# Sums of weight blocks kept in half tiles: four writes a pair instead of eight, and a new order for the whole program

## The chip, the core and the metric

The kernel runs on one core of a Trainium2 chip. The metric is the device time of one execution in microseconds (us). A NeuronCore has five engines, each with its own queue of instructions that it works through in order: TensorE (PE, matmuls), VectorE (DVE), ScalarE (ACT), GpSimd (POOL) and SyncE (SP, which here only issues DMA transfers). Engines wait for one another through semaphores. An instruction that waits holds up everything behind it on its queue.

## The reference, cut to what matters

```python
# q, k, v: (8, 8, 576, 64); w_in: (512, 2048); w_out: (2048, 512)
q_s = exp(q - max(q, -1)); q_s /= sum(q_s, -1) + 1e-9        # softmax over the head's width
k_s = exp(k - max(k, 2));  k_s /= sum(k_s, 2) + 1e-9         # softmax over the sequence
x   = q_s @ (k_s^T @ v)                                      # linear attention, per head
h   = x.reshape(4608, 512) @ w_in
g   = h * tanh(softplus(h))                                  # Mish
out = g @ w_out
```

All of it is in 32-bit floats. The kernel multiplies in a reduced matmul format (fp32r): every operand is split into a high part and a low part, and a product is three matmuls (high x high, high x low, low x high).

## The kernel before, in words

**Stages.** The 4608 rows of x are cut into nine blocks of 512. The first three blocks are multiplied plainly: for each of 16 slices f of the hidden width, `HM` (twelve matmuls of 512 columns, tile `ph`) makes h, `Y` applies Mish, `GA` and `GL` split it into `gh` and `gl`, and `OP` (four parts of three matmuls, tiles `po`) adds to the output. Step number n = 16 x block + f, so `HM16` begins the second block. The last six blocks are done in three rounds (k = 0, 1, 2) of two, by a scheme that makes a 2 x 2 block product with seven block multiplications instead of eight. `Ak.n.p` is one first product (six matmuls) and `BBk.f.p` one second product (six matmuls); `C`, `J`, `N` take results out of PSUM into tiles `g`; `GX` forms differences of such tiles, `GH` and `GK` split them for the second product. `XA`, `XH`, `XL` do the same to x.

**The weights' sums.** The scheme needs, beside the weight blocks themselves, sums and differences of them (products p = 5, 6, 7 and 3). All blocks are written once, in the order in which they will be used, to a scratch tensor `ws` in HBM, and fetched from there in each round by `F` (512 KB each, issued by POOL into a ring of six tiles; two products use up one tile). From the second plain block to the first part of round 0 the kernel fills `ws`:

- `WKj` (16 of them) writes three blocks as they are: three writes of 256 KB on SP, from tiles `wi` or `wo`.
- `WWj` (POOL, two additions) makes the whole values of the pair j of weight tiles, in a tile `w_in` or `w_out` of which there is one buffer only (tag `raw`).
- `WMj` (POOL, four additions of 256 columns) makes the four sums in a tile `m_in` or `m_out` (tag `st`, two buffers).
- `WHj` (ACT) rounds the four sums to their high part and puts it where the whole values stood; `WLj` (DVE) leaves the low part in `m`.
- `WPj` writes them: for each of the four sums its high part and its low part apart, eight writes of 128 KB on SP.

Pairs 0 to 7 are of w_in, 8 to 15 of w_out (`w_out5` is pair 13).

**Attention beside it.** Heads come in pairs. For a pair of tiles, SP loads k (`LK`, tile `kt_two`), v (`V`) and q (`LQ`, one buffer, so a load waits until `EQ` has read the one before). DVE takes the maximum of k (`MK`, tile `km`) and of q (`MQ`, tile `qm`); POOL subtracts (`SQ`) and normalizes (`QM`, tile `qe`); DVE joins sums (`QV`) and transposes q (`T`, tile `qT`); PE multiplies q with the pair's k^T v (`PX`) and makes the next pair's k^T v (`PK`). `ES` and `ST` write finished outputs and leftovers of x.

**What sets the order.** Every engine's order is the order of tokens in two long strings, `FIRST` and `LATER`, which a planner wrote; nothing is reordered afterwards. The tiles `g` of the rounds lie in the memory of the tiles `wo`, so `C0.2.3`, which writes the memory of `wo7`, has to wait for `WW15`, which reads `wo7`.

Of the kernel before, what the change touches and what calls it, by code (L numbers as in the profile page):

```python
# [46 lines left out]
UE8.1 GL16 OP14.0 U8.1 OP14.1 WK5 OP14.2 Y17 LK10 OP14.3 WK9 QW8 HM18g GA17 QV8 WK15 MS9 GL17 QM8 WH0 WK7 MT9 PK6ef T8
SQ9 Y18 WK10 OP15.0 GA18 WL0 OP15.1 V10 OP15.2 EV0.0v WP0 EQ9 OP15.3 GL18 EV0.1s HM19h Q9 EV0.2v QW9 LQ10 MK10 ES0.0
EV0.3s WK12 OP16.0 QV9 OP16.1 OP16.2 WK13 S8 QM9 Y19 OP16.3 KB10 MQ10 ES0.1 WW1 HM20g GA19 T9 MS10 GL19 KM10 OP17.0
WK14 WM1 OP17.1 ES0.2 OP17.2 UE10.0 OP17.3 UE10.1 HM21h MT10 U10.0 SQ10 U10.1 Y20 ES0.3 WH1 LK12 OP18.0 OP18.1 GA20  # L50
WL1 Y21 OP18.2 OP18.3 GL20 WP1 PX8ef EQ10 HM22g GA21 Q10 Z8 LQ11 GL21 Z9 ZL8 QW10 ZL9 QV10 PK8ef WW2 MK12 Y22 OP19.0
V12 ZT8 GA22 ST8 OP19.1 MQ11 ZT9 OP19.2 KB12 ST9 GL22 QM10 OP19.3 MS11 S10 HM23h WM2 OP20.0 Y23 OP20.1 MT11 T10 SQ11
WH2 OP20.2 OP20.3 GA23 KM12 WL2 HM24g GL23 WP2 EQ11 UE12.0 Q11 OP21.0 QW11 U12.0 OP21.1 LQ12 QV11 OP21.2 QM11 OP21.3
Y24 HM25h T11 WW3 UE12.1 MQ12 GA24 U12.1 OP22.0 MS12 OP22.1 GL24 LK14 WM3 OP22.2 OP22.3 Y25 PX10ef GA25 HM26g MT12 WH3
GL25 SQ12 Z10 WL3 Z11 OP23.0 ZL10 WP3 OP23.1 ZL11 EQ12 OP23.2 MK14 OP23.3 HM27h LQ13 Q12 Y26 KB14 GA26 KM14 QW12 GL26
PK10ef WW4 Y27 OP24.0 V14 OP24.1 OP24.2 UE14.0 QV12 WM4 OP24.3 GA27 MQ13 HM28g ZT10 ZT11 ST10 GL27 MS13 ST11 S12
UE14.1 QM12 WH4 OP25.0 OP25.1 MT13 WL4 OP25.2 OP25.3 Y28 SQ13 T12 WP4 HM29h GA28 U14.0 GL28 EQ13 U14.1 OP26.0 LQ14 Q13
LK16 OP26.1 OP26.2 Y29 OP26.3 WW5 QW13 HM30g GA29 QV13 WM5 OP27.0 GL29 Y30 OP27.1 MQ14 GA30 OP27.2 GL30 MS14 OP27.3
MK16 QM13 HM31h WH5 WL5 KB16 T13 WP5 OP28.0 Y31 OP28.1 MT14 KM16 GA31 SQ14 OP28.2 GL31 OP28.3 PX12ef UE16.0 HM32g EQ14
XR12 LQ15 Q14 WW6 XR13 QW14 OP29.0 UE16.1 OP29.1 PK12ef F0 QV14 WM6 MQ15 Y32 OP29.2 V16 ZT12 S14 OP29.3 GA32 ST12  # L60
# [15 lines left out]
C0.0.0 XL0.4 OP47.0 OP47.1 SQ21 T20 A0.0.7 EV2.0v F6 J0.0.0 ES2.0 WW13 A0.0.6 EQ21 EV2.1s LQ22 OP47.2 C0.0.2 ES2.1
OP47.3 KM22 F7 A0.1.1 Q21 WM13 EV2.2v N0.0.0 A0.1.2 ES2.2 QW21 MQ22 C0.1.0 A0.0.5 EV2.3s F8 QV21 WH13 ES2.3 A0.1.7 F9
J0.1.0 QM21 C0.0.3 A0.1.6 MS22 F10 WL13 F11 T21 WP13 UE22.0 J0.0.3 PX20df C0.1.2 U22.0 A0.0.3 UE22.1 MT22 SQ22 XR20
U22.1 A0.0.4 XR21 LK24 EQ22 A0.2.1 F12 J0.0.2 LQ23 WW14 Q22 A0.2.2 N0.0.1 C0.2.0 A0.1.5 QW22 J0.2.0 F13 N0.1.0 QV22
A0.2.7 WM14 N0.2.0 MQ23 C0.1.3 MK24 A0.2.6 MS23 N0.0.2 A0.1.3 J0.1.3 KB24 F14 MT23 QM22 WH14 PK20df C0.2.2 KM24 F15  # L80
WL14 A0.1.4 N0.1.1 V24 ZT20 SQ23 T22 ZT21 WP14 A0.3.1 J0.1.2 UE24.0 A0.3.2 S22 F16 C0.3.0 ST20 U24.0 A0.2.5 EQ23 ST21
J0.3.0 UE24.1 LQ24 A0.3.7 Q23 F17 U24.1 WW15 A0.3.6 N0.3.0 LK26 QW23 MQ24 C0.3.2 N0.1.2 F18 QV23 WM15 C0.2.3 MS24
J0.2.3 A0.2.3 N0.0.3 A0.2.4 N0.1.3 N0.2.1 MT24 QM23 MK26 WH15 A0.4.1 F19 N0.2.3 J0.2.2 A0.4.2 SQ24 C0.4.0 T23 KB26
A0.3.5 F20 J0.4.0 WL15 A0.4.7 EQ24 KM26 WP15 C0.3.3 Q24 PX22df F21 UE26.0 J0.3.3 A0.4.6 QW24 XR22 QV24 A0.3.3 LQ25
XR23 QM24 C0.4.2 A0.3.4 F22 PS PK22df N0.3.1 J0.3.2 GH0.1.0 MQ25 A0.5.1 V26 T24 MS25 A0.5.2 ZT22 F23 MT25 C0.5.0 S24
ST22 SQ25 ZT23 A0.4.5 GH0.1.1 ST23 GK0.1.0 A0.5.7 F24 J0.5.0 GX0.0.0p EQ25 A0.5.6 U26.0 C0.4.3 LQ26 Q25 UE26.1 A0.4.3
J0.4.3 C0.5.2 F25 U26.1 QW25 A0.4.4 GK0.1.1 LK28 A0.6.1 F26 J0.4.2 N0.4.1 GX0.1.0p N0.4.0 A0.6.2 C0.6.0 N0.5.0 A0.5.5
N0.2.2 F27 QV25 GH0.1.2 A0.6.7 J0.6.0 QM25 C0.5.3 MQ26 A0.6.6 N0.6.0 J0.5.3 F28 MS26 T25 A0.5.3 N0.3.2 GK0.1.2 C0.6.2
A0.5.4 N0.4.2 F29 MT26 N0.5.1 GX0.0.1v N0.3.3 A0.7.1 N0.4.3 SQ26 J0.5.2 N0.5.3 A0.7.2 MK28 C0.7.0 F30 GX0.2.0p PX24df
A0.6.5 EQ26 XR24 LQ27 GX0.1.1v A0.7.7 XR25 F31 C0.6.3 J0.7.0 A0.7.6 J0.6.3 N0.5.2 A0.6.3 Q26 F32 C0.7.2 MQ27 N0.7.0  # L90
A0.6.4 GX0.2.1v N0.6.1 GH0.1.3 BB0.0.1 F33 J0.6.2 QW26 GK0.1.3 PK24df MS27 QV26 BB0.1.1 N0.6.2 V28 MT27 ZT24 QM26 S26
ZT25 ST24 KB28 A0.7.5 ST25 GH0.2.0 KM28 F34 T26 SQ27 BB0.2.1 C0.7.3 GK0.2.0 BB0.3.1 F35 UE28.0 J0.7.3 A0.7.3 GH0.2.1
U28.0 A0.7.4 EQ27 GK0.2.1 F36 LQ28 BB0.4.1 Q27 N0.7.1 J0.7.2 BB0.5.1 QW27 GX0.3.0p N0.7.2 BB0.6.1 N0.6.3 GH0.2.2 F37
QV27 BB0.7.1 F38 N0.7.3 GK0.2.2 BB0.0.2 QM27 UE28.1 BB0.1.2 F39 GX0.3.1v GH0.2.3 BB0.2.2 GH0.7.0 T27 BB0.3.2 GK0.2.3
DP0.0.0 F40 DP0.0.1 GK0.7.0 XH1.1 BB0.4.2 GH0.7.1 U28.1 BB0.5.2 F41 GX0.0.2v LK30 PX26df GH0.7.2 GK0.7.1 BB0.6.2 XR26
# [897 lines left out]
```

## Time and profile before

| | |
|---|---|
| median of three runs | 835.33 us (834.29 to 836.96) |
| the profiled execution | 835.84 us, of it 834.1 us span from first to last instruction |
| mean granted TensorE clock | 0.981 of full speed |
| busy: PE, DVE, ACT, POOL | 797.3, 518.5, 536.4, 338.1 us |
| HBM read and written | 138.19 and 39.85 MB |

Shares of the span are means over stages with different limits. The plain blocks end and the rounds begin at about 336 us; a PE that is "busy" has a matmul under way, so what matters for the end is each stretch in which PE stands still, and who ended it. In the views, a name such as `DVE gl L218` is an instruction by its engine, the tile that it writes and its line; L218 is a helper's line, shared by many. `SPq` is SP's queue; the time of an SP entry is the time it took to issue, not to land.

### The profile page before, as it was taken

To read this page: it belongs to the slowest core of one execution; us is meant where nothing else is said; L and a number is where in the kernel's file an instruction comes from. 1 tells how busy PE (TensorE), PEld (TensorE's weight loads), DVE (VectorE), ACT (ScalarE), POOL (GpSimd) and SP (SyncE) were. 2 spreads that over 40 slices of the span, in tenths; PEclk is the share of its full clock that TensorE was granted. 3 is DMA by queue.
4 is the path that set the end of the run, shared out by engine and by line. 5 is a ranking of instruction groups with operands and counts; after the bars stand their busy time and mean duration, and the time that the engine had idled before them with its cause. 6 is when DMAs were issued, how large, how long until landed. Compare 5 with 4: busy or idle time off the path is not lost.

```text
span 834.1 us, 12849 instructions
## 1 busy us (share of the span) xinstructions
PE 797.3 (96%) x4654; PEld 639.6 (77%) x4654; DVE 518.5 (62%) x804; ACT 536.4 (64%) x962; POOL 338.1 (41%) x391
## 2 busy tenths in 40 slices
PE   9899999399999999896999999999999999999998
...
PEclk9999999699999999988999999999999999999999
...
GB/s 343 392 325 146 56 129 332 341 206 144 132 223 138 134 152 100 274 264 250 262 217 223 261 189 254 251 195 195 205 201 210 217 232 205 195 201 183 221 198 180
DMA packets 85758, 178.87 MB, mean 214 GB/s; under 512 B 16576, under 2 KB 45248, under 8 KB 85696
## 3 DMA queue, kind: packets, MB, share of 16 engines
...
HBM read 138.19 MB, written 39.85 MB: 213 GB/s over the span
## 4 chain that ended last, share of the span: by engine, by line
PE 77%; DMA 7%; SPq 5%; ACT 4%; POOL 3%; DVE 2%; issue 2%; POOLq 0%; ACTq 0%; DVEq 0%
PE px L805 13%; PE ph L619 12%; PE qx L822 12%; PE po L657 11%; PE qz L822 8%; PE qy L822 8%; PE py L805 7%; SPq L693 4%; PE pz L805 3%; PE px L524 1%; DMA kt<-in_kt_dram 1%; POOL m_out L725 1%; DMA raw_x<-in_w_dram 1%; DMA ws<-w_out 1%; POOL w_out L715 1%
## 5 line engine op out<-in xcount | busy, mean ns | idle before, releaser
L788 POOL DMA_DIRECT2D ws<-ws x172 | 93.2, 542 | 299.1 <-PE qx L822 66.8
L855 ACT CAST gs<-g 128x1024 fp32r<-128x1024 f32 x84 | 88.3, 1052 | 85.4 <-PE qx L822 38.7
L805 PE MATMUL px<-xh,ws 128*128 128x512 f32 x384 | 134.0, 397 | 7.9 <-ACT g L833 7.9
L218 DVE TENSOR_TENSOR gs<-g,gs 128x1024 fp32r<-128x1024 f32 x84 | 105.1, 1251 | 45.3 <-ACT gs L855 44.9
L657 PE MATMUL po<-wo,gh 128*128 128x512 f32 x384 | 119.6, 393 | 0.0
L822 PE MATMUL qx<-gs,ws 128*128 128x512 f32 x432 | 100.7, 389 | 0.0
L619 PE MATMUL ph<-xs,wi 128*128 128x512 f32 x384 | 96.8, 399 | 1.3 <-ACT qT L516 1.2
L805 PEld LDWEIGHTS px<-xh,ws 128*128 128x128 f32 x384 | 73.3, 191 | 28.1 <-ACT g L833 8.7
L822 PEld LDWEIGHTS qx<-gs,ws 128*128 128x128 f32 x432 | 81.0, 188 | 16.9
L619 PEld LDWEIGHTS ph<-xs,wi 128*128 128x128 f32 x384 | 71.8, 191 | 19.6 <-issue 2.0
L657 PEld LDWEIGHTS po<-wo,gh 128*128 128x128 f32 x384 | 71.2, 188 | 18.1 <-issue 3.2
L805 PE MATMUL px<-xl,ws 128*128 128x512 f32 x192 | 75.7, 394 | 0.0
L657 PE MATMUL po<-wo,gl 128*128 128x512 f32 x192 | 74.7, 389 | 0.0
L841 ACT ACTIVATE g<-g 128x512 f32<-128x512 f32 x72 | 44.8, 631 | 44.8 <-DVE g L837 44.4
L837 DVE TENSOR_TENSOR g<-py,g 128x512 f32<-128x512 f32 x48 | 32.9, 684 | 63.7 <-PE py L805 48.7
L805 PE MATMUL py<-xh,ws 128*128 128x512 f32 x192 | 68.3, 397 | 0.0
L822 PE MATMUL qy<-gs,ws 128*128 128x512 f32 x288 | 67.2, 389 | 0.0
L822 PE MATMUL qz<-gs,ws 128*128 128x512 f32 x288 | 67.0, 389 | 0.0
L822 PEld LDWEIGHTS qz<-gs,ws 128*128 128x128 f32 x288 | 54.0, 188 | 12.0 <-issue 0.8
L619 PE MATMUL ph<-xs_odd,wi 128*128 128x512 f32 x192 | 48.8, 405 | 14.9 <-DVE gl L218 14.9
L833 ACT COPY g<-px 128x512 f32<-128x512 f32 x72 | 41.9, 582 | 32.9 <-PE px L805 28.6
L822 PEld LDWEIGHTS qy<-gs,ws 128*128 128x128 f32 x288 | 54.0, 188 | 11.2
...
## 6 DMA issues: line engine op xcount, KB each, us to landing
...
v<-in_v_dram SPq DMA_DIRECT2D x14, 594.0 KB, 4.6
...
kt_two<-in_kp_dram SPq DMA_DIRECT2D x12, 576.0 KB, 4.3
q<-in_qs_dram SPq DMA_DIRECT2D x24, 288.0 KB, 3.4
ws<-wi SPq DMA_DIRECT2D x24, 256.0 KB, 3.7
ws<-wo SPq DMA_DIRECT2D x24, 256.0 KB, 4.1
out_dram<-ob SPq DMA_DIRECT2D x24, 256.0 KB, 3.8
```

The source lines that it names most:

```text
L218: eng.tensor_tensor(out, a, b, ALU.subtract)
L524: nc.tensor.matmul((px, pt)[x][h][o], kvt[a, j], at[e + j]["qT"][x][a], start=True, stop=True)
L619: nc.tensor.matmul(gs[n], wi[f][:, a, t], x[:, z], start=t == 0 and i == 0, stop=t == HP - 1 and i == 2)
L657: nc.tensor.matmul(po[t], g[a][:, t * P:(t + 1) * P], wo[f][:, z], start=f == 0 and i == 0, stop=f == NF - 1 and i == 2)
L693: nc.sync.dma_start(dst if z is None else dst[:, z], src)
L788: nc.gpsimd.dma_start(t.rearrange("p s z j c -> p s (z j c)"), ws[e % (NW // 2)].bitcast(F32R))
L805: nc.tensor.matmul(dst, w[:, a, j], xc[k, p][z][:, j].rearrange("p b s -> p (b s)"), start=p in (1, 2, 7) and j == 0 and i == 0, stop=j == ...
L822: nc.tensor.matmul(psb[key, k][m], w[:, a, m], g[:, z, f % 2], start=first and i == 0, stop=f == NH - 1 and i == 2, skip_group_check=p in ...
L833: nc.scalar.copy(g_quad(k, n)[q], psb[1, k, n])
L837: nc.vector.tensor_tensor(g, psb[2 if q == 0 else 7, k, n], g, ALU.add)
L841: nc.scalar.activation(g, psb[1, k, n] if q == 1 else g, AF.Mish)
L855: nc.scalar.copy(t[:, 0], gq[k, h][G_PART[p]])
```

## The change

A pair's four sums are made, split and written in two halves s = 0 (p = 5, 6) and s = 1 (p = 7, 3). Each half has a tile `m0` or `m1` of the same tag and size as before, in which high and low part lie side by side for each sum, as `ws` wants them. So a sum is one write of 256 KB, and a pair is four writes instead of eight. The high part no longer goes over the whole values: the one buffer of `raw` is free once `WMj.1` has read it, and not only when eight writes have landed; in its place each pair takes both buffers of `st`. `WMj.1` reads a sum of `m0`, and so stands ahead of `WLj.0`, which overwrites it. `WH` and `WL` are two instructions of half the size each.

```diff
-    def w_mix(j, eng="p"):
+    def w_mix(j, s, eng="p"):
...
-        m = pools["wp"].tile([P, 4, 2 * P], F32, tag="st", name=f"m_{kind}{f}")
-        for o, x, y, op in ((0, a21, a22, ALU.add), (1, m[:, 0], a11, ALU.subtract),
-                            (2, a11, a21, ALU.subtract), (3, a12, m[:, 1], ALU.subtract)):
-            engines[eng].tensor_tensor(m[:, o], x, y, op)
-        mixed[j] = a.rearrange("p j h e -> p (j h) e"), m
+        m = mixed[j, s] = pools["wp"].tile([P, 2, 2, 2 * P], F32, tag="st", name=f"m{s}_{kind}{f}")
+        if s == 0:
+            pairs = (m[:, 0, 1], a21, a22, ALU.add), (m[:, 1, 1], m[:, 0, 1], a11, ALU.subtract)
+        else:
+            pairs = (m[:, 0, 1], a11, a21, ALU.subtract), (m[:, 1, 1], a12, mixed[j, 0][:, 1, 1], ALU.subtract)
+        for d, x, y, op in pairs:
+            engines[eng].tensor_tensor(d, x, y, op)
 
-    def w_mix_hi(j):
-        a, m = mixed[j]
-        nc.scalar.copy(a.bitcast(F32R), m)
+    def w_mix_hi(j, s):
+        m = mixed[j, s]
+        nc.scalar.copy(m[:, :, 0].bitcast(F32R), m[:, :, 1])
 
-    def w_mix_lo(j, eng="v"):
-        a, m = mixed[j]
-        sub(engines[eng], m.bitcast(F32R), m, a)
+    def w_mix_lo(j, s, eng="v"):
+        m = mixed[j, s]
+        sub(engines[eng], m[:, :, 1].bitcast(F32R), m[:, :, 1], m[:, :, 0])
 
-    def w_mix_out(j):
+    def w_mix_out(j, s):
         kind, f = kinds[j]
-        a, m = mixed.pop(j)
-        for i, p in enumerate((5, 6, 7, 3)):
-            w_put((1 if kind == "in" else 2, p, f), 0, a[:, i])
-            w_put((1 if kind == "in" else 2, p, f), 1, m[:, i])
+        m = mixed[j, s]
+        for i, p in enumerate(((5, 6), (7, 3))[s]):
+            w_put((1 if kind == "in" else 2, p, f), None, m[:, i])
...
-WW0 KB8 WK0 HM16g WM0 WK1 WK2 OP13.0 WK4 OP13.1 KM8 Q8 WK6 OP13.2 Y16 MQ9 OP13.3 WK3 HM17h WK8 UE8.0 WK11 GA16 U8.0
+WW0 KB8 WK1 HM16g WM0.0 KM8 WH0.0 WM0.1 Q8 WK0 UE8.0 OP13.0 OP13.1 MQ9 WW1 UE8.1 OP13.2 U8.0 WK2 OP13.3 U8.1
```

`FIRST` is the same in both. `LATER` is ordered anew throughout, and the twelve `GX` that POOL did (four in each round) go to DVE. The order moves instructions on every engine; three places follow.

SP, from the start of the second plain block to the load of q10 (`in_qs_dram`; `wi` and `wo` are `WK`, `w_in` and `m_in` are `WP`). Before, 39 writes of `WK`, a load of k, a load of v and eight writes of `WP0` stand ahead of it, of which this is the end:

```order
L693 DMA ws<-wi_96 128x2x256 x2
L693 DMA ws<-wi_104 128x2x256
L693 DMA ws<-wo_618 128x2x256
L693 DMA ws<-wo_1019 128x2x256 x2
L344 DMA v_113<-in_v_dram 128x1188
L693 DMA ws<-w_in_1458 128x256
L693 DMA ws<-m_in_1482 128x256
...
L334 DMA q_1711<-in_qs_dram 128x576
```

Now fifteen writes of `WK`, the load of k and two writes of `WP0.0` stand ahead of it. These are all of them but the first three writes:

```order
L698 DMA ws<-wi_89 128x2x256 x2
L698 DMA ws<-wi_97 128x2x256
L698 DMA ws<-wi_91 128x2x256 x2
L698 DMA ws<-wi_99 128x2x256
L328 DMA kt_two<-in_kp_dram 128x1152
L698 DMA ws<-m_in_1482 128x512 x2
L698 DMA ws<-wi_92 128x2x256 x2
L698 DMA ws<-wi_100 128x2x256
L698 DMA ws<-wi_93 128x2x256 x2
L698 DMA ws<-wi_101 128x2x256
L339 DMA q_1610<-in_qs_dram 128x576
```

So the load of q10 moves ahead of 24 writes of `WK`, of the load of v and of the second half of pair 0's sums; the writes that it passed now stand between later loads.

DVE, at the start of round 0, around the transposes of q21 (`qT21`) that `PX20` on PE needs. Before:

```order
L380 TENSOR_REDUCE qm22_3804<-q22_3761 128x18
L371 TENSOR_TENSOR qs21_3781<-qs21_3781,sz21_3799 128x18
L476 TENSOR_SCALAR qs21_3781,total21_3818<-qs21_3781 128x18
L477 RECIPROCAL qs21_3781<-qs21_3781 128x18
L837 TENSOR_TENSOR g0_0_0_3718<-pz0_1_3791,g0_0_0_3718 128x512
L218 TENSOR_TENSOR m_out5_3783<-m_out5_3783,w_out5_3748 128x1024
L494 STREAM_TRANSPOSE qT21_3851<-qe21_3757 128x512
```

Now:

```order
L385 TENSOR_REDUCE qm22_3783<-q22_3734 128x18
L376 TENSOR_TENSOR qs21_3741<-qs21_3741,sz21_3768 128x18
L481 TENSOR_SCALAR qs21_3741,total21_3799<-qs21_3741 128x18
L482 RECIPROCAL qs21_3741<-qs21_3741 128x18
L223 TENSOR_TENSOR m1_out4_3738<-m1_out4_3738 128x2x256
L843 TENSOR_TENSOR g0_0_0_3688<-pz0_1_3776,g0_0_0_3688 128x512
L453 STREAM_TRANSPOSE k22_3826<-kt_two_114 128x576
L843 TENSOR_TENSOR g0_0_3_3691<-py0_0_3715,g0_0_3_3691 128x512
L499 STREAM_TRANSPOSE qT21_3840<-qe21_3723 128x512
```

The low part of pair 13 (`m_out5`) stood right ahead of the transpose; it now follows it, and the nearest one ahead is the second half of pair 12 (`m1_out4`).

POOL, in round 0, around `WW15` (tile `w_out7`), for which ACT's `C0.2.3` waits. Before:

```order
L481 TENSOR_TENSOR qe22_3895<-qe22_3895,qs22_3912 128x576
L788 DMA ws15_4037<-ws_109 128x1024
L218 TENSOR_TENSOR q23_3907<-q23_3907,qm23_3959 128x576
L788 DMA ws16_4087<-ws_109 128x1024
L788 DMA ws17_4116<-ws_109 128x1024
L715 TENSOR_TENSOR w_out7_4119<-wo7_937 128x512
L715 TENSOR_TENSOR w_out7_4119<-wo15_1424 128x512
L788 DMA ws18_4139<-ws_109 128x1024
```

Now:

```order
L794 DMA ws14_3988<-ws_109 128x1024
L733 TENSOR_TENSOR m0_out6_3995<-w_out6_3878 128x256
L733 TENSOR_TENSOR m0_out6_3995<-m0_out6_3995,w_out6_3878 128x256
L733 TENSOR_TENSOR m1_out6_4013<-w_out6_3878 128x256
L733 TENSOR_TENSOR m1_out6_4013<-w_out6_3878,m0_out6_3995 128x256
L720 TENSOR_TENSOR w_out7_4034<-wo7_937 128x512
L720 TENSOR_TENSOR w_out7_4034<-wo15_1424 128x512
L486 TENSOR_TENSOR qe22_3975<-qe22_3975,qs22_3986 128x576
L794 DMA ws15_4069<-ws_109 128x1024
```

`WW15` moves ahead of `F15` to `F17` and of the work on q22 and q23, right behind the sums of pair 14, whose reading frees its buffer.

More of the change, by code (lines that the diff above doesn't have):

```diff
@@ L45 @@
 LATER = """
-WW0 KB8 WK0 HM16g WM0 WK1 WK2 OP13.0 WK4 OP13.1 KM8 Q8 WK6 OP13.2 Y16 MQ9 OP13.3 WK3 HM17h WK8 UE8.0 WK11 GA16 U8.0
[L47 to L60, printed above, removed]
@@ L76 @@
[L76 to L90, printed above, removed]
@@ L91 @@
[L91 to L95, printed above, removed]
@@ new lines @@
+GL17 WM1.0 EQ9 MK10 LQ10 WH1.0 WP0.1 PK6ef Q9 KB10 WK5 OP15.0 QW9 KM10 S8 OP15.1 OP15.2 EV0.0v OP15.3 QV9 V10 Y18
+ES0.0 HM19h EV0.1s MQ10 QM9 WK8 GA18 EV0.2v WM1.1 MS10 GL18 EV0.3s T9 WK6 OP16.0 WW2 OP16.1 OP16.2 UE10.0 OP16.3 ES0.1
+HM20g MT10 WK7 U10.0 SQ10 Y19 WL1.0 WP1.0 PX8ef UE10.1 WK9 OP17.0 GA19 U10.1 OP17.1 GL19 OP17.2 LK12 OP17.3 Y20 ES0.2
+HM21h Z8 WK11 WM2.0 GA20 ZL8 Z9 GL20 ZL9 WK15 OP18.0 EQ10 OP18.1 Q10 OP18.2 MK12 OP18.3 LQ11 Y21 ES0.3 HM22g QW10 WK10
+GA21 QV10 KB12 GL21 QM10 WH1.1 WK13 OP19.0 KM12 Y22 WL1.1 OP19.1 MQ11 OP19.2 OP19.3 WP1.1 UE12.0 HM23h WK12 GA22 MS11
@@ new lines @@
+QV20 OP45.1 WH11.1 WW12 OP45.2 OP45.3 OP46.0 OP46.1 WL11.0 OP46.2 QM20 WP11.0 OP46.3 A0.0.1 WL11.1 MT21 WP11.1 XA0.3v
+A0.0.2 C0.0.0 SQ21 T20 XH0.4 OP47.0 J0.0.0 OP47.1 F6 WM12.0 EV2.0v A0.0.7 ES2.0 EQ21 A0.0.6 XL0.4 EV2.1s LQ22 WH12.0
+ES2.1 WM12.1 Q21 OP47.2 OP47.3 N0.0.0 A0.1.1 KM22 F7 WL12.0 C0.0.2 F8 EV2.2v WP12.0 QW21 WW13 A0.1.2 MQ22 ES2.2 C0.1.0
+WH12.1 A0.0.5 EV2.3s F9 QV21 ES2.3 A0.1.7 F10 WL12.1 UE22.0 QM21 J0.1.0 WP12.1 A0.1.6 C0.0.3 U22.0 WM13.0 UE22.1
+A0.0.3 J0.0.3 T21 C0.1.2 F11 A0.0.4 WH13.0 U22.1 MS22 LK24 WM13.1 A0.2.1 PX20df MT22 N0.0.1 WW14 J0.0.2 C0.2.0 A0.2.2
@@ new lines @@
+WH13.1 XR20 XR21 F12 WL13.0 N0.1.0 PK20df SQ22 WP13.0 N0.0.2 A0.1.5 N0.0.3 F13 WL13.1 V24 J0.2.0 WP13.1 A0.2.7 S22
+EQ22 C0.1.3 LQ23 A0.2.6 Q22 F14 ZT20 ZT21 ST20 J0.1.3 WM14.0 QW22 A0.1.3 ST21 MK24 C0.2.2 WM14.1 A0.1.4 N0.2.0 QV22
+A0.3.1 WW15 N0.1.1 J0.1.2 KB24 A0.3.2 MQ23 C0.3.0 MS23 KM24 A0.2.5 QM22 J0.3.0 MT23 F15 A0.3.7 T22 UE24.0 SQ23 C0.2.3
+U24.0 A0.3.6 F16 EQ23 F17 J0.2.3 UE24.1 LQ24 A0.2.3 Q23 F18 C0.3.2 U24.1 A0.2.4 QW23 LK26 QV23 A0.4.1 F19 J0.2.2 QM23
+N0.2.1 MQ24 A0.4.2 WH14.0 T23 C0.4.0 A0.3.5 MS24 F20 J0.4.0 WH14.1 MT24 WL14.0 PX22df N0.3.0 SQ24 WP14.0 C0.3.3 A0.4.7
```

147 lines of the change are left out of this document (86 added, 61 removed).

## The prediction

> **What bounds the kernel now.** I read the page's head, then the waits of PE, then the timeline of PE where it stands still.
>
> ```profile
> span 834.1 us, 12849 instructions
> PE   9899999399999999896999999999999999999998
> PEclk9999999699999999988999999999999999999999
> ```
>
> Each digit is a fortieth of the span (20.9 us). PE is busy nearly everywhere; two slices, the eighth and the nineteenth, are not, and the granted clock falls there too.
>
> ```profile
> PE ph L619 <- DVE gl L218: 14.9, 2, 14.0
> PE px L805 <- ACT g L833: 7.9, 2, 6.7
> PE px L524 <- DVE qT L494: 5.0, 2, 4.4
> ...
> 162.60 3.78 PE L619 MATMUL ph<-xs_odd,wi 128*128 128x512 f32 x8 [14.00 <-DVE gl L218]
> 356.28 1.97 PE L524 MATMUL px<-qT,kvt 64*64 64x512 f32 x4 [4.44 <-DVE qT L494]
> 387.49 0.79 PE L805 MATMUL px<-xh,ws 128*128 128x512 f32 x1 [6.65 <-ACT g L833]
> 398.24 1.09 PE L524 MATMUL px<-qT,kvt 64*64 64x512 f32 x8
> 413.22 0.50 PE L805 MATMUL px<-xh,ws 128*128 128x512 f32 x1 [1.23 <-ACT g L833]
> ```
>
> The first rows are PE's waits (total, times, longest), the others its timeline with the idle time in brackets. Four stalls, 14.00 + 4.44 + 6.65 + 1.23 = 26.3 us, all between 148 and 414 us: the stretch in which the weights' sums are written. Behind the three long ones the clock is low too, which the chain of waits shows:
>
> ```profile
> 162.60 5.20 PE ph L619 x12
> 358.25 2.86 PE px L805 x6
> 387.49 2.93 PE px L805 x6
> 421.70 2.72 PE px L805 x12
> ```
>
> Twelve matmuls take 2.72 us at full clock, so the first stall costs 5.20 - 2.72 = 2.5 us more, the second 2.86 - 1.36 = 1.5 and four of L524 1.97 - 0.55 = 1.4, the third 2.93 - 1.36 = 1.6: 7.0 us. The 1.23 us stall is followed by no such slowing. If all four stalls went, 33.3 us would go.
>
> **Stall 1, SP's order.** Timelines of SP's queue and of DVE:
>
> ```profile
> 119.79 13.07 SPq L693 DMA_DIRECT2D ws<-wi  x18
> 150.63 0.66 SPq L344 DMA_DIRECT2D v<-in_v_dram  x1
> 157.29 0.38 SPq L334 DMA_DIRECT2D q<-in_qs_dram  x1
> ...
> 145.45 1.35 DVE L361 TENSOR_REDUCE km<-kt_two 128x4 f32<-128x1152 f32 x1 [7.18 <-DMA kt_two<-in_kp_dram]
> 160.47 0.75 DVE L380 TENSOR_REDUCE qm<-q 128x18 f32<-128x576 f32 x1 [12.40 <-DMA q<-in_qs_dram]
> 161.89 0.65 DVE L218 TENSOR_TENSOR gl<-ph,gh 128x512 fp32r<-128x512 f32 x1
> ```
>
> DVE stands 12.40 us before the maximum of q10, whose load SP issues only at 157.29; `GL19` behind it frees the PSUM bank of `HM21`. What stands ahead of the load is limited by bytes, as the windows (width, five engines' busy time, granted clock, DMA share, GB/s) and the page's table of sizes show:
>
> ```profile
> 119.80:157.30 37.50, 28.80 (x192) 23.39 (x192) 13.24 (x30) 19.20 (x39) 6.76 (x8) 0.95 1.02 334
> 150.00:160.00 10.00, 0.00 (x0) 0.00 (x0) 0.00 (x0) 0.00 (x0) 0.64 (x1) 0.68 0.98 307
> 335.70:412.00 76.30, 65.20 (x411) 49.55 (x409) 42.51 (x85) 53.37 (x108) 41.67 (x52) 0.91 0.84 264
> 410.00:520.00 110.00, 108.77 (x631) 87.73 (x630) 94.69 (x115) 77.90 (x131) 36.91 (x48) 1.00 0.77 228
> ...
> v<-in_v_dram SPq DMA_DIRECT2D x14, 594.0 KB, 4.6
> kt_two<-in_kp_dram SPq DMA_DIRECT2D x12, 576.0 KB, 4.3
> q<-in_qs_dram SPq DMA_DIRECT2D x24, 288.0 KB, 3.4
> ws<-wi SPq DMA_DIRECT2D x24, 256.0 KB, 3.7
> ws<-m_out SPq DMA_DIRECT2D x32, 128.0 KB, 2.8
> out_dram<-ob SPq DMA_DIRECT2D x24, 256.0 KB, 3.8
> ```
>
> 39 x 256 + 576 + 594 + 8 x 128 KB = 12.5 MB in 37.5 us is 333 GB/s, the first window's rate, with all 16 DMA engines busy (share 1.02). In the new order 15 x 256 + 576 + 2 x 256 KB = 5.05 MB stand ahead: issue at 119.8 + 15.1 = 134.9, landing (157.29 to 160.47 before: 3.2) at 138.1. `HM16` starts at 119.7; four `HM` and four `OP` of 2.72 and about 1.2 for `PK6` put `HM20`, whose bank waits behind this `MQ10`, at 142.7. `MQ10` and `GL18` (0.75 + 0.65) are done at 139.5. The stall goes, with 3 us to spare.
>
> The bytes stay the same, so what is late next are the loads behind. k12: 6.41 MB more stand ahead, issue at 154.1, maximum started 5.4 after issue (140.08 to 145.45 before), 159.5; with its 1.35, the join of sums (about 0.7) and `GL21` 162.2. `HM23` could start at 142.7 + 3 x 5.44 + 1.1 (`PX8`) = 160.1: 2.1 us lost. q12: 7.29 MB further, issue 175.9, landed 179.1, maximum and the transposes of q11 behind it (0.75 + 0.9) until 180.7; `PX10` could start at 162.2 + 5 x 2.72 + 1.2 + 1.4 = 178.4: 2.3 us lost. I put back 4.4. Bounds: nothing, if these land a little earlier; at 307 GB/s, the worst ten microseconds above, everything is 8.8% later, k12 costs 5.1 and q12 4.2, each with its low clock (2.5): 14.
>
> [...]
>
> **Stalls 2 and 3, the buffer.** Two stretches of the chain of waits:
>
> ```profile
> 341.41 4.72 DMA ws<-w_out
> 353.39 2.21 DVE m_out L218
> ...
> 381.22 4.25 DMA xt_dram<-xt
> 385.56 1.27 POOL w_out L715
> ```
>
> POOL's `WW13` waits until the writes of pair 12 have landed, since their high parts lie in the one `raw` buffer; then `WM13`, `WH13` and `WL13` follow one another, and `WL13` stands ahead of `qT21` on DVE. In the new order the buffer is free when POOL has read it, `WL13` stands behind `qT21`, and pair 12 is done earlier: the 4.44 go. At the third, `WW15` waits for transfers (the row names the leftovers' write; by the code it is pair 14's writes, issued just before), and `C0.2.3` waits for `WW15`. `WW15` now needs no landing and stands some four first products (1.36 each) ahead of `C0.2.3`: the 6.65 go. The 1.23 hung on a load of q behind `WP15`, now ahead of both halves of it: gone.
>
> What is late next: 264 GB/s over 76.3 us are 20.1 MB; at share 0.84 that is 314 GB/s when full, so 64.2 us. PE's 65.2 busy us hold 4.5 us of low clock: 60.7. DMA is short by about 3.5 us. `F` runs five tiles ahead (13.6 us), so PE need not wait for it, but loads and landings shift. I put back 3.0; bounds 0 and 7 (3.5 in one piece, with its low clock).
>
> **The rest.** POOL's `WM` now waits for both `st` buffers of the pair before: a 256 KB write lands in 3.8 us instead of 2.8 for 128 KB, and behind `WM` on POOL stand `QM`, `SQ` and `F`. In the plan three to four products of 1.36 lie between, and hardly anything waits; bounds 0 and rival B's 11. SP saves 64 issues of some 0.4 us, on a queue that is not late outside the two stretches: nothing. Splitting and moving:
>
> ```profile
> L855 ACT CAST gs<-g 128x1024 fp32r<-128x1024 f32 x84 | 88.3, 1052 | 85.4 <-PE qx L822 38.7
> L637 ACT CAST gh<-ph 128x512 fp32r<-128x512 f32 x39 | 22.8, 584 | 1.2 <-PE po L657 0.6
> L218 DVE TENSOR_TENSOR g<-g,g 128x1024 f32<-128x1024 f32 x36 | 47.4, 1322 | 10.7 <-POOL g L218 10.3
> ...
> 428.14 2.39 POOL L218 TENSOR_TENSOR g<-g,g 128x1024 f32<-128x1024 f32 x1
> 427.69 3.94 DVE L218 TENSOR_TENSOR g<-g,g 128x1024 f32<-128x1024 f32 x1
> ```
>
> Two halves on ACT are 2 x 584 - 1052 = 116 ns more a pair, 1.9 us over 16 pairs in 250 us: hidden by ACT's idle time. Four `GX` more on DVE add 4 x 1.32 = 5.3 us a round; in round 0 DVE is busy 94.7 of 110 us (the window from 410), so they fit, with 10 us left. The last two rows show that they may cost less: the same operation took 3.94 us instead of 1.32 on DVE while POOL ran one. The Trainium skill, "GPSIMD Engine Reference", Specifications, says that POOL shares its SBUF interfaces with DVE and contends with DVE instructions that have two SBUF inputs; by that rule an estimate would be a gain of DVE time, not a loss. PE's matmuls are the same in number.
>
> **The sum.** Against the profiled execution: 835.84 - 26.3 - 7.0 + 4.4 + 3.0 = 809.9. That execution is 0.5 us above the median of the runs; I say 810.
>
> **The rivals.**
> A, DMA is the wall: the bytes stay, the loads behind arrive as at 307 GB/s and the round's start loses its 7. For it: shares of 0.98 to 1.02 for 37 us. Against: before, DMA ran nearly empty after 180 us, so the new order has room to lend. It puts back 14 + 6 = 20: 835.8 - 33.3 + 20 = 822.5 at its worst, some 819 in the middle.
> B, the wait moves into the ring of `st`: POOL stands in `WM` until writes land, and `QM` and with it `qT` come late for the eleven pairs from `PX10` to `PX30`, 1 us each: 810 + 11 = 821. For it: each landing is on POOL's path; against: POOL is busy 338 of 834 us.
> C, DVE becomes the bound in the rounds, the other side: `GX` moved to DVE and pushed later (from `F24`-`F36` to `F29`-`F40` in round 0) lie among the `GK` that `BB` needs. It decides where DVE's 5.3 us more exceed its 15 idle us per 110. To end slower than before it has to give back 26 us, 9 in each round: about 839. For it: DVE at 86% in round 0. Against: the later rounds have no attention beside them in their second half.
> D, nothing is gained: the load of q10 is early, but the next one holds PE as long: 835. Against: it would have to lie 14 us later than its bytes say.
>
> **How the numbers follow.** The forecast, 802 to 814, has 0.63; A (814 to 823) 0.20; B 0.08; D 0.04; C 0.05. A difference of 0.3% (2.5 us) is about what a measurement of this kernel can tell from none. Faster 0.91, same 0.04, slower 0.05. The low end is the sum with almost nothing put back (802.5) and a microsecond for the clock; the high end is A at its worst. The range leaves out C, D and the tail of B.
>
> **What would show it.** Right: no wait of PE above 3 us between 148 and 414 us, the maximum of q10 at about 138; small waits near `HM23` and `PX10`; POOL's waits for landed writes at `WM` and not at `WW`; 64 x 128 rows, and so 8192 packets, fewer. Wrong: a wait of PE over 4 us on `GL` or `qT` in the first stretch (A), many of 1 us on `qT` (B), waits of `qx`, `qy` or `qz` on DVE `gs` after 450 us (C).

## The result, and the profile after

The changed kernel takes 808.75 us (median, 806.55 to 810.37), the kernel before on the same chip 834.81 (834.1 to 836.96): a ratio of 0.9682, interval 0.9651 to 0.9713. On a second chip, beside the experiments, it was 0.9678 (0.9650 to 0.9706). The forecast was 810, with a chance of 0.63 on 802 to 814; with rival A the range went from 801.5 to 823. The profiled execution took 807.92 us. The page's head:

```profile
span 806.2 us, 12794 instructions
PE   9999999999999999899999999999999999999998
PEclk9999999999999999999999999999999999999999
DMA packets 76542, 178.86 MB, mean 222 GB/s; under 512 B 15552, under 2 KB 27840, under 8 KB 76480
```

The two slices in which PE stood still are full, and so is the clock; the bytes are the same in 9216 packets fewer (85,758 before). 8192 of them were forecast; the other 1024 are all under 512 B (15,552 now, 16,576 before) and come to 16 for each of the 64 writes saved. PE's waits from 120 us on, in its timeline:

```profile
176.11 0.65 PE L529 MATMUL px<-qT,kvt 64*64 64x512 f32 x2 [0.16 <-DVE qT L499]
340.64 0.33 PE L529 MATMUL pt<-qTt,kvt 64*64 64x64 f32 x2 [2.35 <-ACT raw L760]
358.95 0.50 PE L811 MATMUL px<-xh,ws 128*128 128x512 f32 x1 [1.05 <-ACT g L839]
393.77 0.50 PE L811 MATMUL px<-xh,ws 128*128 128x512 f32 x1 [1.78 <-ACT g L839]
```

None of the four old stalls is there. In the first stretch 0.3 us are left (0.16 here and 0.15 at 147.27), around the start of round 0 another 5.3 (a second 0.16 stands at 341.13), and 0.58 at 514.71. SP's queue, and DVE's maxima of q10, k12 and q12:

```profile
130.55 1.43 SPq L339 DMA_DIRECT2D q<-in_qs_dram  x1
136.05 0.69 DVE L385 TENSOR_REDUCE qm<-q 128x18 f32<-128x576 f32 x1
154.88 1.35 DVE L366 TENSOR_REDUCE km<-kt_two 128x4 f32<-128x1152 f32 x1 [2.42 <-DMA kt_two<-in_kp_dram]
174.69 0.75 DVE L385 TENSOR_REDUCE qm<-q 128x18 f32<-128x576 f32 x1 [2.12 <-DMA q<-in_qs_dram]
```

The load of q10 issues 26.7 us sooner than before (23.8 when both are counted from the start of `HM16`, as below), and its maximum no longer waits. DVE still waits 2 us for k12 and q12, but PE behind it does not.

**How much of it is chance.** `HM16` is the first step whose order the change touches; all before it is `FIRST`, the same in both. It starts here, in the kernel before, in the first profile after and in the second:

```profile
119.67 3.02 PE L619 MATMUL ph<-xs_odd,wi 128*128 128x512 f32 x12 [0.92 <-DVE gl L218]
...
116.74 3.02 PE L624 MATMUL ph<-xs_odd,wi 128*128 128x512 f32 x12 [0.92 <-DVE gl L223]
...
119.80 3.01 PE L624 MATMUL ph<-xs_odd,wi 128*128 128x512 f32 x12 [0.92 <-DVE gl L223]
```

Over all profiles of this study it lies between 116.7 and 119.8, whatever the kernel. So 2.9 us of the first difference are the luck of one execution, and kernels are better compared from `HM16` to the end: 834.1 - 119.7 = 714.4 before, 806.2 - 116.7 = 689.5 and 808.1 - 119.8 = 688.3 after: 24.9 and 26.1 us less. The prediction had 33.3 - 7.4 = 25.9. This measure has a spread of its own: two kernels of the same median below, 811.15 and 811.26, differ by 4.6 us in it.

### The profile page after: what moved, and what is told of

Same layout as the page of the kernel before. It is cut to its first block, busy times and chain, and to the rows that moved or that the text cites. A ratio compares the mean times of both kernels' runs of the same rounds, so it can differ in the third digit from the quotient of the medians.

```text
span 806.2 us, 12794 instructions
## 1 busy us (share of the span) xinstructions
PE 791.2 (98%) x4654; PEld 634.8 (79%) x4654; DVE 531.1 (66%) x832; ACT 545.1 (68%) x984; POOL 314.4 (39%) x379
## 2 busy tenths in 40 slices
DMA packets 76542, 178.86 MB, mean 222 GB/s; under 512 B 15552, under 2 KB 27840, under 8 KB 76480
## 4 chain that ended last, share of the span: by engine, by line
PE 75%; DMA 10%; POOL 4%; ACT 4%; DVE 3%; issue 3%; SPq 1%; POOLq 0%; ACTq 0%; DVEq 0%
PE ph L624 13%; PE po L662 13%; PE qx L828 12%; PE px L811 11%; PE qz L828 8%; PE qy L828 7%; PE py L811 5%; DMA ws<-m_out 3%; DMA q<-in_qs_dram 3%; PE pz L811 2%; PE px L529 1%; DMA raw_x<-in_w_dram 1%; PE pt L567 1%; POOL m_out L733 1%; DMA kt<-in_kt_dram 1%
## 5 line engine op out<-in xcount | busy, mean ns | idle before, releaser
L811 PE MATMUL px<-xh,ws 128*128 128x512 f32 x384 | 132.2, 392 | 3.4 <-ACT g L839 3.4
L223 DVE TENSOR_TENSOR g<-g,g 128x1024 f32<-128x1024 f32 x48 | 60.3, 1265 | 17.9 <-ACT g L847 17.6
L223 POOL TENSOR_TENSOR q<-q,qm 128x576 f32<-128x576 f32 (+1 forms) x32 | 39.9, 1250 | 50.5 <-PE ph L624 19.6
```

The lines of the kernel that those rows point to most:

```text
L223: eng.tensor_tensor(out, a, b, ALU.subtract)
L811: nc.tensor.matmul(dst, w[:, a, j], xc[k, p][z][:, j].rearrange("p b s -> p (b s)"), start=p in (1, 2, 7) and j == 0 and i == 0, stop=j == ...
```

## The experiments

Twelve runs in four groups, each group on one chip beside the kernel before. "From HM16" is the span of the profiled execution less the start of `HM16`, to be held against 714.4 before. That 714.4 is from the first chip, where the kernel before had a median of 834.81; beside the four groups it had 837.8 to 838.2, and no profile of it was taken there. So a saving against 714.4 may be some 3 us too small, and where the two columns differ the ratio is the safer one.

| kernel | median us | ratio to before (95%) | from HM16 |
|---|---|---|---|
| q10 early, whole tiles | 830.59 | 0.990 (0.985 to 0.995) | 709.1 |
| the same, and T21 ahead of WL13 | 831.42 | 0.992 (0.989 to 0.995) | 709.7 |
| half tiles, old order | 825.26 | 0.986 (0.978 to 0.995) | 706.2 |
| q10 and q11 early, whole tiles | 828.46 | 0.990 (0.986 to 0.993) | 707.9 |
| q10 and q11 early, half tiles | 817.03 | 0.975 (0.972 to 0.978) | 696.7 |
| changed kernel again | 811.15 | 0.968 (0.965 to 0.971) | 688.3 |
| changed, 128 KB writes | 815.06 and 814.89 | 0.972 (0.967 to 0.977), 0.972 (0.968 to 0.975) | 695.4, 692.4 |
| changed, GX back on POOL | 811.26 | 0.968 (0.965 to 0.971) | 692.9 |
| changed, three places of ACT | 809.26 | 0.965 (0.962 to 0.968) | 692.0 |
| round 0's start, PK20 behind V24 | 810.17 | 0.966 (0.963 to 0.969) | 692.6 |
| round 0's start | 805.10 | 0.961 (0.959 to 0.964) | 682.2 |

**1. SP's order alone.** Whole tiles; the sixteen `WK` and `V10` stand where the new order has them, and:

```diff
-GA18 WL0 ... WP0 EQ9 OP15.3 ... Q9 EV0.2v QW9 LQ10
+GA18 EQ9 LQ10 WL0 ... WP0 OP15.3 ... Q9 EV0.2v QW9
```

> The kernel before with whole tiles and eight writes a pair; only the sixteen WK, V10 and the load of q10 (with EQ9 ahead of it) stand where the new order has them. Theory 'SP's order alone makes stall 1': the 14.0 us wait and its 2.5 us of low clock go, stalls 2 to 4 (4.44, 6.65, 1.23) stay as they are; 834.8 - 16.5 + 1 = about 819 (817 to 821). Rival 'the smaller writes hold DMA at 334 GB/s': the loads of k12 and q12 land as late as the prediction had it and put 4.4 back: about 823. Rival 'half tiles are needed': a wait of more than 8 us on gl stays: 830 or more.

Measured: 0.990, 830.6 us. DVE and PE, in their timelines:

```profile
171.73 0.75 DVE L380 TENSOR_REDUCE qm<-q 128x18 f32<-128x576 f32 x1 [8.84 <-DMA q<-in_qs_dram]
173.13 0.80 PE L619 MATMUL ph<-xs_odd,wi 128*128 128x512 f32 x1 [6.29 <-DVE gl L218]
349.57 1.12 PE L524 MATMUL px<-qT,kvt 64*64 64x512 f32 x2 [5.76 <-DVE qT L494]
379.99 0.80 PE L805 MATMUL px<-xh,ws 128*128 128x512 f32 x1 [5.83 <-ACT g L833]
```

The wait of 14 us at q10 is gone with the order alone, but 6.3 of it come back at the next load, q11, which still stood behind pair 1's eight writes and nine of `WK` and was issued at 167.95. The first theory has the cause of stall 1 and misses the time (0.981 was expected, some 9 us less); the last comes near the time, but no wait of 8 us is left. It is rival D's mechanism at half its size. Stalls 2 and 3 stay.

**2. Stall 2 by order.** As 1, and at pair 13:

```diff
-Q21 WM13 ... QV21 WH13 ... QM21 ... WL13 F11 T21
+Q21 ... QV21 QM21 WM13 WH13 ... T21 WL13 F11
```

> As the kernel with q10 loaded early, and besides, at pair 13: QM21 ahead of WM13 on POOL, and T21 ahead of WL13 on DVE. Whole tiles still. Theory 'stall 2 is a place in two queues': qT21 is there some 3.6 us earlier, the 4.44 becomes about 0.8, and its low clock (2.9) goes: about 6 less than that kernel. But WM13 now waits for QV21, so pair 13's writes leave 2 to 3 us later and stall 3 (6.65) can grow by as much: 813 to 816. Rival 'only the free buffer helps': stall 2 keeps more than 3 us, and the time is that of the kernel with q10 early, or longer.

Measured: no gain on kernel 1 (831.4 against 830.6 us), where about 6 us were expected. PE's timeline:

```profile
345.41 0.65 PE L524 MATMUL px<-qT,kvt 64*64 64x512 f32 x2 [1.20 <-DVE qT L494]
349.07 0.50 PE L805 MATMUL px<-xh,ws 128*128 128x512 f32 x1 [2.59 <-ACT g L833]
365.44 0.50 PE L805 MATMUL py<-xh,ws 128*128 128x512 f32 x1 [2.23 <-DVE g L837]
381.44 0.79 PE L805 MATMUL px<-xh,ws 128*128 128x512 f32 x1 [6.90 <-ACT g L833]
```

5.76 became 1.20 at its place, as the theory said, and 2.59, 1.68 (2.23 for 0.55) and 1.07 more at stall 3 took its room. While a whole pair has to land before the next one starts, this order only moved the wait.

**3. The half tiles alone.**

```diff
-WMj ... WHj ... WLj ... WPj
+WMj.0 WMj.1 ... WHj.0 WHj.1 ... WLj.0 WLj.1 ... WPj.0 WPj.1
```

> The half tiles with four writes a pair, in the order of before: each WMj, WHj, WLj, WPj is replaced where it stands by its two halves; GX stays on POOL as before. Theory 'the one buffer makes stalls 2 and 3': WW13 and WW15 no longer wait for landed writes, stall 2 goes from 4.44 to about 1, stall 3 from 6.65 to about 1.4, with 2.9 and 1.6 of low clock; stall 1 (14.0) stays, since what stands ahead of q10's load has the same bytes: about 822 (820 to 825). Rival 'the wait only moves': WM13.0 and WM15.0 stand right behind WW13 and WW15 and wait for the ring of st just as long; stalls 2 and 3 stay: 832 to 836. Rival 'fewer writes matter by themselves': stall 1 shrinks by over 2 us.

Measured: 0.986. From HM16 on 8.2 us less. PE's timeline and POOL's only wait for a ring of `st` (total, times, longest):

```profile
160.12 0.79 PE L623 MATMUL ph<-xs_odd,wi 128*128 128x512 f32 x1 [13.54 <-DVE gl L222]
374.47 0.50 PE L810 MATMUL px<-xh,ws 128*128 128x512 f32 x1 [3.15 <-ACT g L838]
...
POOL m_in L732 <- DMA ws<-m_in: 13.9, 4, 6.8
```

Stall 1 stays (13.54), stall 2 has no row any more, stall 3 is halved: the buffer theory, with stall 3 less reduced than forecast, since `WW15` now waits for its place behind an `F`. Stall 1 did not shrink by 2 us, so fewer writes alone do not lift it. No `WM` of the last eight pairs waits for a landing, so the wait did not just move.

**4. The next load too.** Kernel 1 with EQ10 and LQ11 ahead of WL1, then the same with half tiles:

```diff
-GA20 WL1 Y21 OP18.2 OP18.3 GL20 WP1 PX8ef WK9 EQ10 HM22g WK10 WK13 GA21 Q10 Z8 LQ11
+GA20 EQ10 LQ11 WL1 Y21 OP18.2 OP18.3 GL20 WP1 PX8ef WK9 HM22g WK10 WK13 GA21 Q10 Z8
```

> As the kernel with q10 loaded early (whole tiles, eight writes), with the load of q11 and EQ10 also moved, ahead of pair 1's eight writes and of the writes of WK that stood before it. There, q11 was issued at 168.0 and landed at 171.7, and HM23 waited 6.3 us with 2.8 of low clock behind it. Theory 'stall 1 had moved to the next load': q11 is issued at about 161, that wait goes to under 1 us, and the time falls by 6 to 9: about 0.980 of before. Rival 'the rate is short for the whole stretch': k12 or q12 waits instead, 3 us or more, and the time falls by less than 4.

> The kernel with q10 and q11 loaded early, now with the half tiles and four writes a pair, expanded in place in the old order; GX stays on POOL. Theory 'two independent parts': the half tiles take off what they did in the old order (12 us: stall 2, half of stall 3 and low clock), the two loads what they do with whole tiles (13 to 16): 0.966 to 0.972, as good as the changed kernel, without its new order for the rest. Rival 'the parts need each other or the rest of the new order': 0.976 or more.

Measured with whole tiles: 0.990, as kernel 1, where 0.980 was expected. Two waits came instead; the first is neither k12's nor q12's. POOL, PE and DVE:

```profile
164.36 1.29 POOL L715 TENSOR_TENSOR w_in<-wi 128x512 f32<-128x512 f32 x1 [16.96 <-DMA ws<-wo]
...
173.90 0.50 PE L619 MATMUL ph<-xs_odd,wi 128*128 128x512 f32 x1 [3.10 <-DVE gl L218]
184.41 0.51 PE L619 MATMUL ph<-xs_odd,wi 128*128 128x512 f32 x1 [2.12 <-DVE gl L218]
...
182.34 0.75 DVE L380 TENSOR_REDUCE qm<-q 128x18 f32<-128x576 f32 x1 [3.23 <-DMA q<-in_qs_dram]
```

With q11 there, POOL's `WW2` stands 17 us before the one buffer, whose writes by the code are pair 1's; `WM2`, `WH2` and `WL2` follow, and `GL23` behind `WL2` on DVE frees the bank that PE waits 3.10 us for. So the one buffer holds the first stretch as well, hidden before by the longer wait. The 2.12 stand behind the maximum of q12, whose load is late, as the rival had it, though by less than 3 us. After each of the two, twelve matmuls take 4.6 us instead of 3.0. With half tiles the wait of 3.10 is gone, and one of 3.60 for q12 is left, with no slow matmuls behind it:

```profile
182.26 0.50 PE L623 MATMUL ph<-xs_odd,wi 128*128 128x512 f32 x1 [3.60 <-DVE gl L222]
```

In this stretch the two parts need each other: the half tiles alone leave a wait of 13.54, the two loads alone 3.10 and 2.12 with slow matmuls behind both, together they leave 3.60. Over the whole kernel that does not show. From HM16 on the parts bring 8.2 and 6.5 us and both together 17.7, but the medians say 1.4% and 1.0% and together 2.5%, which is their sum, with intervals of plus or minus 0.3 to 0.8% each; and PE's waits of over 0.14 us from 120 us on, 26.9 in all before, fall by 5.3 and 8.9, and together by 13.5. The expectation of 0.966 to 0.972 was too good, since it had 13 to 16 us for the loads. The changed kernel has another 7 to 8 us from HM16 on; its order for q12's load and at stall 3 and `GX` are the differences, and none of them was tried alone here.

**5. The size of a write.** The changed kernel with high and low part written apart:

```diff
-            w_put((1 if kind == "in" else 2, p, f), None, m[:, i])
+            for z in range(2):
+                w_put((1 if kind == "in" else 2, p, f), z, m[:, i, z])
```

> The changed kernel, with each sum written as two writes of 128 KB (high and low part apart) instead of one of 256 KB: 64 more writes, 8192 more packets, the same bytes, the same order. Theory 'bytes, not writes': the same time within 0.3% (806.5 to 811). Rival 'the rate': the rate between 118 and 160 us falls from 352 to about 334 GB/s, k12 and q12 land 3 to 5 us later and HM23 and PX10 wait about 2 us each, as the prediction had it: 812 to 814.

> The changed kernel with 128 KB writes again, now on the same chip as the changed kernel itself. The first run put PX10's wait at 2.0 us, and the rate between 140 and 160 us at 341 GB/s where the changed kernel had 378. Theory 'the size of a write sets the rate': 0.3 to 0.8% slower than the changed kernel, with 2 us at PX10 and 1 to 2 us more at the start of round 0. Rival 'chance, or another chip': within 0.3%.

> The changed kernel once more, as the base for the runs beside it: about 0.968 of the kernel before. The start of the program, whose code and order are the same in both, was 2.9 us shorter in its profile than in that of before (HM16 at 116.7 against 119.7); if that is chance, HM16 starts anywhere between 116.7 and 119.7 here, and PE's waits from 120 us on (0.2, 0.2, 2.5, 1.1, 1.8, 0.6) are as in the first profile within 1 us each. If the change causes it, it starts at 117 or earlier.

PE at `PX10` in its two runs, and in the changed kernel again:

```profile
180.33 0.65 PE L529 MATMUL px<-qT,kvt 64*64 64x512 f32 x2 [2.01 <-DVE qT L499]
...
178.36 0.65 PE L529 MATMUL px<-qT,kvt 64*64 64x512 f32 x2 [1.41 <-DVE qT L499]
...
179.14 1.08 PE L529 MATMUL px<-qT,kvt 64*64 64x512 f32 x4 [0.30 <-DVE qT L499]
```

Windows of 37 us, from 1 us after the start of `HM16` (last column GB/s): the changed kernel twice, then small writes twice.

```profile
117.74:154.74 37.00, 36.85 (x230) 28.91 (x229) 21.17 (x42) 31.64 (x62) 16.53 (x18) 1.00 1.04 347
120.80:157.80 37.00, 36.87 (x231) 29.07 (x230) 21.20 (x42) 31.80 (x62) 16.52 (x18) 1.00 1.04 348
...
120.11:157.11 37.00, 36.87 (x230) 28.91 (x229) 21.17 (x42) 31.65 (x62) 16.51 (x18) 1.00 1.04 334
118.81:155.81 37.00, 36.84 (x230) 28.98 (x229) 20.53 (x42) 31.73 (x62) 17.10 (x18) 1.00 1.03 335
```

Theory "bytes, not writes" fails: 815 us, above both ranges of the first expectation. The medians lie 0.5% apart on one chip (814.89 and 811.15), though the intervals of the ratios overlap. At `PX10` small writes cost 1.1 to 1.9 us more, twice; PE's waits of over 0.14 us from 120 us on add up to 10.5 and 9.4 us with them, and to 6.2 and 4.8 without, most of the rest around the start of round 0. In this stretch the size acts through the rate: 334 and 335 GB/s against 347 and 348, and the maximum of q12 starts 59.8 and 59.1 us after `HM16` instead of 58.0 and 57.9. The windows must be counted from `HM16`: a fixed one from 140 to 160 us, as in the expectation, falls on other work whenever the start of the program is 3 us longer.

**6. GX.** `GX0.0.0v` to `GX2.3.0v`, twelve of them, back to `p`.

> The changed kernel with the twelve GX that the change moved to DVE back on POOL, at the same places in the order. Theory 'off the path': no wait of PE appears from 400 us on, within 0.3% of the changed kernel. Rival 'POOL slows DVE': a DVE subtraction of 1.32 us takes up to 3.94 beside a GX on POOL; if it is one that BB waits for, 12 x 2.6 = up to 31 us of DVE time more, of which some 3 to 8 us reach PE, as waits of qx on gs. Rival 'DVE was the tighter one': faster by 2 to 5 us, with less of the waits of px on g in round 0.

Measured: 811.26 us, the changed kernel's 811.15. Groups of DVE with GX on POOL, then all on DVE:

```profile
L222 DVE TENSOR_TENSOR gs<-g,gs 128x1024 fp32r<-128x1024 f32 x84 | 108.7, 1298 | 45.8 <-ACT gs L860 45.4
...
L223 DVE TENSOR_TENSOR gs<-g,gs 128x1024 fp32r<-128x1024 f32 x84 | 104.0, 1240 | 46.3 <-ACT gs L861 45.9
```

POOL's twelve cost DVE's `GK` 58 ns each on the mean, 4.7 us in all, on an engine that has room: off the path. DVE is busy 521.1 us in all with GX on POOL and 531.1 without, so the move costs DVE time and does not gain it, as the estimate in the prediction had it.

**7. What is left at round 0.** First three places of ACT:

```diff
-WH13.1 XR20 XR21 ... T22 UE24.0 SQ23 C0.2.3 ... UE26.0 GK0.1.0 A0.6.6 F28 C0.5.3
+XR20 XR21 WH13.1 ... T22 C0.2.3 UE24.0 SQ23 ... C0.5.3 UE26.0 GK0.1.0 A0.6.6 F28
```

> The changed kernel with three places of ACT's order changed: XR20 and XR21 ahead of WH13.1, C0.2.3 ahead of UE24.0, C0.5.3 ahead of UE26.0. They aim at what is left of PE's waits at the start of round 0: 2.35 + 0.16 on ACT raw, 1.05 and 1.78 on ACT g, 5.3 us in all, and some 0.8 of low clock behind the first. Theory 'ACT's order makes them': 5 to 6 us less than the changed kernel, about 0.961 of before. Rival 'something behind them is late as well' (WH13.1 and the exponentials come later, with pair 13's writes and the next k^T v): 0 to 3 us less, with waits of the same sum at PX22 or C0.3 to C0.6.

Measured: 0.965, 1.9 us less than the changed kernel where 5 to 6 were expected, and within the intervals. PE, and what its second wait goes back to on POOL:

```profile
342.29 0.27 PE L528 MATMUL pt<-qTt,kvt 64*64 64x64 f32 x1 [1.80 <-ACT raw L759]
350.21 0.50 PE L810 MATMUL px<-xh,ws 128*128 128x512 f32 x1 [1.76 <-ACT g L838]
363.21 0.50 PE L810 MATMUL py<-xh,ws 128*128 128x512 f32 x1 [1.82 <-DVE g L842]
398.33 0.50 PE L810 MATMUL py<-xh,ws 128*128 128x512 f32 x1 [1.81 <-DVE g L842]
...
342.27 0.71 POOL L732 TENSOR_TENSOR m_out<-w_out 128x256 f32<-128x256 f32 x1 [3.90 <-DMA ws<-m_out]
```

The rival: other waits of the same size. The second is rival B's mechanism of the prediction: `WM13.1` waits 3.90 for the ring of `st`, `SQ22` comes late behind it (347.80), `EQ22` and `C0.1.3` behind that. So `SQ22` goes ahead of `WW14`, `C0.1.3` ahead of `EQ22`, the `J` right behind their `C`, and `PK20`, which needs the banks that `XR20` and `XR21` empty, two products later.

```diff
-MT22 N0.0.1 WW14 ... PK20df SQ22 ... V24 J0.2.0 WP13.1 A0.2.7 S22 EQ22 C0.1.3
+MT22 SQ22 N0.0.1 WW14 ... J0.2.0 WP13.1 A0.2.7 PK20df V24 S22 C0.1.3 EQ22
```

> The changed kernel with more of round 0's start reordered: besides the three places on ACT (XR20, XR21, C0.2.3, C0.5.3 earlier), PK20 two first products later on PE, SQ22 ahead of WW14 on POOL, C0.1.3 ahead of EQ22, and J0.2.3 and J0.5.3 right behind their C. The three places alone left waits of 1.80 + 0.17 (raw), 1.76 (C0.1.3 behind EQ22 behind SQ22 behind the ring of st), 1.82 and 1.81 (J behind transposes that wait for exponentials) and gave 0.9653. Theory 'these are single places in queues': all five go, 6 us less: about 0.958. Rival 'the ring and the loads of q pace the whole stretch': the waits move on to qT22 and qT23 (PX22) or C0.3, and it stays at 0.963 to 0.966.

> The kernel with round 0's start reordered, with V24 put behind PK20: in the run before, PK20 stood behind the load of pair 24's v and waited 5.9 us for it, while of the five waits aimed at only 1.3 and 0.4 us were left. Theory 'single places in queues': without that wait 5.9 us and some 0.9 of low clock less than 0.9656 of before: about 0.958. Rival 'the load of q and the ring pace the stretch': a wait of 3 us or more appears at PX22 or behind C0.3, and it stays at 0.963 or more.

In the first of the two, V24 kept its place ahead of `PK20`, so that `PK20` reads pair 24's v instead of pair 22's and waits for that load; it does not compute the reference, and stands here only as a step. The second has the order shown. PE in the first and then in the second, the only wait that its timeline shows after 150 us:

```profile
348.85 0.39 PE L566 MATMUL pt<-v,k 64*64 64x66 f32 x4 [5.89 <-DMA v<-in_v_dram]
...
364.77 0.65 PE L528 MATMUL px<-qT,kvt 64*64 64x512 f32 x2 [1.64 <-DVE qT L498]
```

0.961, or 805.1 us, where 0.958 was expected: below the changed kernel's 0.968 with intervals apart. The waits were single places in queues. This is the fastest version of the study.

## Why the prediction was right, and where it was not

**The sum.** From HM16 on, 25.9 forecast, 24.9 and 26.1 measured. What was to be removed was right; that the total is so near is luck, since two errors of about 4 us in what was put back cancel.

**Removed: 33.3.** The four stalls went as named, 26.3. That the causes are the ones named is shown by kernel 1 (stall 1 goes with SP's order, and stays at 13.54 without it in kernel 3) and kernel 3 (stall 2 goes with the buffer, stall 3 falls to 3.15). The 1.23 was not tried alone. The low clock was put a little high: four matmuls of L524 with idle time ahead take 1.08 at full clock (the row of `PX10` above), not 0.55, so 6.5 and not 7.0. What the prediction lacked is how the two causes hang together: it took stall 1 as SP's matter alone. With whole tiles, wait after wait appears in its place (q11 with 6.29, then `WW2` with 3.10 and q12 with 2.12); the half tiles, which it gave to stalls 2 and 3, are what lifts the one at `WW2`.

**Put back in stretch 1: 4.4, measured 0.3 and 0.3.** The step that failed is the term for k12 and q12. Counted from HM16, the maximum of k12 was forecast at 159.5 - 119.7 = 39.8 and came at 38.1 (154.88 - 116.74); that of q12 at 59.4 and came at 58.0. SP issued both loads sooner than counted: k12 32.3 us after `HM16` and not 34.4, q12 52.4 and not 56.2 (q12 then took 5.5 us to its maximum, not 3.2). The rate of the old order was too low a guide: in the window of kernel 5 it moves 339 GB/s, and the new order 347 and 348. With 128 KB writes the new order moves 334 and 335, k12 is issued at 33.5 both times, and the wait at `PX10` is 2.01 and 1.41, near the forecast 2.3. And PE was later than counted by hand. `HM23` was counted at 40.4 without loss and came at 41.5. `PX10` was counted at 58.7, which holds k12's 2.1, so at 56.6 without loss; it began at 58.1, and only its second half, at 59.4, needs the transposes behind q12's maximum:

```profile
174.88 1.08 PE L529 MATMUL px<-qT,kvt 64*64 64x512 f32 x4
```

Loads 1.4 to 1.7 us sooner and PE 1.1 and 2.8 later leave 0.3 of two waits of 2.

**Put back in round 0: 3.0, measured 5.9 and 4.5 of waits, with low clock.** Windows from 335 to 400 us, the changed kernel twice, then the last version:

```profile
335.00:400.00 65.00, 59.55 (x399) 45.62 (x398) 41.82 (x82) 52.35 (x108) 33.82 (x42) 0.97 0.85 275
335.00:400.00 65.00, 61.02 (x406) 46.78 (x405) 42.54 (x83) 52.90 (x113) 34.52 (x43) 0.97 0.86 287
...
335.00:400.00 65.00, 63.27 (x429) 48.42 (x428) 44.20 (x85) 56.65 (x117) 36.32 (x45) 1.00 0.90 295
```

The mechanism was wrong: not DMA short of bytes. The same transfers flow faster (295 GB/s, clock 1.00) once ten steps stand in another order. The waits were on `XR` ahead of `PK20` and on `C` behind exponentials, which the prediction did not look for. The clock of 0.97 costs about 0.03 x 65 = 1.9 us. The account closes: 26.3 + 6.5 - 0.3 - 5.9 - 1.9 = 24.7, against 24.9 measured.

**Costed at nothing.** GX on DVE: right for PE (kernel 6). SP's fewer issues and ACT's 2 x 584 ns: nothing of them shows on PE's path, though writes of half the size cost about 0.5% (kernel 5). The ring of `st` "hardly waits": wrong for POOL, right for PE. POOL's waits, before and after:

```profile
POOL w_in L715 <- DMA ws<-w_in: 42.8, 6, 10.7
POOL w_out L715 <- DMA ws<-w_out: 15.9, 3, 10.8
...
POOL m_out L733 <- DMA ws<-m_out: 20.4, 7, 8.3
POOL m_in L733 <- DMA ws<-m_in: 16.0, 9, 3.8
```

They moved from `WW` to `WM`, as said, and fell from 59 to 36 us in these rows (42 in the changed kernel's second profile); one of them reached PE when the others were cleared (kernel 7).

**The rivals.** A did not come: no wait over 0.3 us on `gl` or `qT` in the first stretch. B is there in kind, worth under 2 us. C: no wait of `qx`, `qy` or `qz` on `gs`. D's mechanism shows in kernel 1, at half its size (6.29). A's worst case adds 14 + 6 though the round's bound is 7; that changes its price by 1 us. The Trainium skill, "DMA: Bandwidth & Descriptors", Bandwidth, has about 358 GB/s as what each of two cores gets that stream from one HBM domain at the same time. This kernel runs on one core, and that figure is no ceiling for it: from 23.3 to 43.3 us after `HM16` it moved 378 and 372 GB/s in its two runs, 363 and 358 with the smaller writes.
